# Row sums, the rounding of x and two weight conversions moved between engines in the start of a banded-attention and gated-FFN kernel

## The chip, the cores and the metric

The kernel runs on one core of one Trainium2 chip. The metric is the device time of one execution in microseconds (us), as the median of several runs. The core has five engines that each work through a queue of their own: TensorE (PE; its weight loads are shown apart as PEld), VectorE (DVE), ScalarE (ACT), GpSimd (POOL) and SyncE (SP), which here issues all DMAs.

## The reference

Attention over eight batches of 576 positions with eight heads of 64, in which each position sees itself and the 63 before it, and then a gated feed-forward network over the 4608 rows that come out:

```python
scores = 1 / np.sqrt(D) * np.matmul(q, k.transpose(0, 1, 3, 2))
rel = pos[:, None] - pos[None, :]
mask = (rel >= 0) & (rel < 64)
scores = np.where(mask, scores, -1000000000.0)
attn = np.exp(scores - np.max(scores, axis=-1, keepdims=True))
attn = attn / (np.sum(attn, axis=-1, keepdims=True) + 1e-09)
out = np.matmul(attn, v)                       # heads are put side by side: x is 4608 x 512
gate = 1.0 / (1.0 + np.exp(-(x @ w_gate)))     # 512 x 1536
return (gate * (x @ w_val)) @ w_out            # 1536 x 512
```

All weights come in as 64-bit numbers. The matrix products need more precision than one pass of the matrix engine gives, so every operand is split into a rounded high part and a low remainder, and each product is made of three matmuls: high by high, high by low, low by high.

## The kernel before

The 4608 rows are cut into 12 tiles of 384. A tile's attention is done in four units, one for each pair of heads: unit (t, p) is pair p of tile t. A unit goes through these steps:

- `scores` (line 224): 24 small matmuls into two banks, one for each head.
- `exponentials` (lines 235 to 260): six times VectorE adds the mask and takes the row's extreme (line 249), and ScalarE makes the exponential (line 257). For head 0 the exponential also accumulates its row sum; for head 1 of the first two tiles it doesn't.
- `normalize` (lines 267 to 274): for head 1 of the first two tiles VectorE sums the rows in an operation of its own (line 270); then it inverts the sums (lines 264 and 265), and GpSimd multiplies (line 274).
- `stage_b` (lines 319 to 333): TensorE transposes (line 324), and ScalarE copies the result out (line 329, tiles `pT0` and `pT1`).
- `stage_c` (lines 335 to 342): TensorE multiplies with v (line 354, tile `oo`); for the first two tiles `x_split` (lines 359 to 364) rounds the result to x's high part on ScalarE (line 361) and takes the low remainder on VectorE (line 362).

The weights come in slabs: number i is slab j, kind m of w_gate, w_val and w_out (0, 1, 2). A slab is loaded as 64-bit words by SyncE (`raw`, line 105). `conv_a` on ScalarE turns the high words into `w32` (line 117) and the low words, in place, into whole numbers (line 118). `conv_b` on VectorE puts the two together (lines 126 to 130). `conv_c` rounds the high part on ScalarE (line 158) and takes the remainder on VectorE (line 159), and SyncE stores the parts and `w32` for later tiles (lines 474 and 154). There are six buffers for `raw` and three for `w32`, so the fourth slab's `w32` can be written when the first one's store has been read out, and so on.

The first two tiles go through the network with their weights as these come (lines 376 to 440: `up` for the two products with x, at line 387, and `down` for the third, at line 435). The other ten tiles use a scheme with fewer products (line 612), which takes most of the time.

The order of the work is set in two steps. A list of events with due times (from line 731 on) fixes the order in which the program is written, and matmuls keep that order. A scheduler then orders each other engine's queue by its own forecast of when things are ready. `tc.issue_after(ins)` holds back what is written under it: it is queued behind `ins` on the engine on which `ins` itself stands, and on that engine alone. Lines 951 to 955 use this for the weights: slab 3 (gate, second) goes behind the two instructions that `x_split` noted for unit (1, 1), and slabs 2, 4 and 5 behind those of unit (1, 3) (`marks`, line 363). One of the two is the rounding at line 361, the other the remainder at line 362.

Of the kernel before, what the change touches and what calls it, by code (L numbers as in the profile page):

```python
# [14 lines left out]
AF = mybir.ActivationFunctionType  # L15
ALU = mybir.AluOpType
# [10 lines left out]
def attn_ffn(ctx: ExitStack, tc: tile.TileContext, qT, kT, vN, w_gate, w_val, w_out, out, outT):  # L27
# [3 lines left out]
    nc = tc.nc  # L31
# [56 lines left out]
    def table_order():  # L88
        return tc.issue_after(chain[-1]) if chain else nullcontext()
# [18 lines left out]
    def conv_a(i):  # L108


        j, m = divmod(i, KINDS)
        raw = conv[i]
        hw = raw.bitcast(F32).rearrange("p (n two) -> p n two", two=2)[:, :, 1]
        lw = raw.bitcast(U32).rearrange("p (n two) -> p n two", two=2)[:, :, 0]
        r32 = raw.bitcast(I32).rearrange("p (n two) -> p n two", two=2)[:, :, 0]
        w32 = mp.tile([P, DM], F32, name=f"w32_{m}_{j}", tag="w32", bufs=W32)
        nc.scalar.activation(w32, hw, AF.Copy, scale=2.0 ** -112)
        nc.scalar.activation(r32, lw, AF.Copy, scale=2.0 ** -29)
        conv[i] = (r32, w32)

    def conv_b(i):
# [107 lines left out]
    def softmax(t, p):  # L229
        sc = sc_of.pop((t, p))  # L230
        for h in range(2):
            exponentials(t, p, h, sc[h])
            normalize(t, p, h)

    def exponentials(t, p, h, sc):
        g0 = order[t] * UT
        if t < 2 and (NP * t + p) % 3 == 2:
            pt = mp.tile([P, TT], F32, name=f"p{h}_{t}_{p}", tag=("hh", "hl")[h], bufs=3)
            pt = pt.rearrange("p (u c) -> p u c", u=UP)
        else:  # L240
            pt = ap.tile([P, UP, P], F32, name=f"p{h}_{t}_{p}", tag="p", bufs=4)
        mn = sm.tile([P, UP], F32, name=f"mn{h}_{t}_{p}", tag="mn")
        if h == 0:
            sums_of[(t, p)] = sm.tile([P, 2, UP], F32, name=f"rs_{t}_{p}", tag="rs")
        rs = sums_of[(t, p)][:, h, :]
        for u in range(UP):
            key = [int((g0 + 2 * u + s) % SEQ == 0) for s in range(2)]
            key = tuple(key[::-1] if h else key)
            nc.vector.tensor_tensor_reduce(out=pt[:, u, :], in0=sc[u], in1=masks[key],  # L249
                                           op0=ALU.add, op1=ALU.min, scale=-SCALE, scalar=3.0e38,  # L250
                                           accum_out=mn[:, u:u + 1])
            with ExitStack() as behind:
                behind.enter_context(table_order())
                if NP * t + p - 2 in marks["pT"] and (t, p) != (1, NP - 1):
                    behind.enter_context(tc.issue_after(marks["pT"][NP * t + p - 2]))
                sums = {} if t < 2 and h else {"accum_out": rs[:, u:u + 1]}
                exp = nc.scalar.activation(pt[:, u, :], pt[:, u, :], AF.Exp, bias=mn[:, u:u + 1],  # L257
                                           scale=-1.0, **sums)
            chain.append(exp.ins)
        st[(t, p, h)] = pt  # L260

    def invert(rs):

        nc.vector.scalar_tensor_tensor(out=rs, in0=rs, scalar=2e-9, in1=rs, op0=ALU.add, op1=ALU.add)  # L264
        nc.vector.reciprocal(out=rs, in_=rs)  # L265

    def normalize(t, p, h):
        pt, rs = st[(t, p, h)], sums_of[(t, p)][:, h, :]
        if t < 2 and h:
            nc.vector.reduce_sum(out=rs, in_=pt, axis=mybir.AxisListType.X)  # L270
        if t < 4:
            invert(rs)
        eng = nc.vector if t == 3 and p % 2 or t // 2 == 2 else nc.gpsimd
        eng.tensor_mul(out=pt, in0=pt, in1=rs.unsqueeze(2).broadcast_to([P, UP, P]))  # L274
# [3 lines left out]
    def stage_s(t, p, done=None, spare=None):  # L278
        if done:
            sc = [a_bank(f"s{h}_{t}_{p}") for h in range(2)]  # L280
            sc_of[(t, p)] = [pieces(b) for b in sc]
            piece, start = spare_up(spare)
            oo = [sc[0][:, UP, :], sc[1][:, UP, :], piece]
            outputs(*done, oo, (True, True, start))
            x = xf_tile(*done).rearrange("p (u c) -> p u c", u=UP)
        scores(t, p)
        sc = sc_of.pop((t, p))
        if done:
            nc.scalar.copy(x[:, 2, :], oo[2])
            nc.scalar.copy(x[:, 1, :], oo[1])  # L290
        exponentials(t, p, 0, sc[0])
        if done:
            nc.scalar.copy(x[:, 0, :], oo[0])
        exponentials(t, p, 1, sc[1])
# [19 lines left out]
    def stage_n(t, p):  # L314
        invert(sums_of[(t, p)])
        for h in range(2):
            normalize(t, p, h)
# [17 lines left out]
    def stage_c(t, p):  # L335
        oo = bank(t, p, "o", f"oo_{t}_{p}")
        outputs(t, p, [oo[:, u, :] for u in range(UP)])
        oo = oo.rearrange("p u c -> p (u c)")
        if t < 2:
            xs[(t, p)] = x_split(oo, f"{t}_{p}", 4 * t + p, nc.vector)  # L340
        else:
            marks["xf"] = nc.scalar.copy(xf_tile(t, p), oo).ins
# [15 lines left out]

    def x_split(src, nm, i, eng):
        x2 = xp.tile([P, 2, TT], F32R, name=f"x_{nm}", tag=f"x{i}")  # L360
        hi = nc.scalar.copy(x2[:, 0, :], src)
        lo = eng.tensor_sub(out=x2[:, 1, :], in0=src, in1=x2[:, 0, :].bitcast(F32))  # L362
        marks[nm] = (hi.ins, lo.ins)
        return x2
# [146 lines left out]
    sums = {}  # L511
# [240 lines left out]
    for n in range(2 * NP):  # L752
        t, p = divmod(n, NP)
# [54 lines left out]
    for i in range(KINDS * NF):  # L808
        j, m = divmod(i, KINDS)
        tm = at[("up", 0, max(j, 1))] + ((-10, -2, 6 * j - 0.5) if j < 2 else (-9, -8, 2) if j == 2 else (-14, -12, 2))[m]  # L810
        if i < 2:
            tm = A0 + 11 + 8 * i
        else:
            put(tm - (30 if j == 0 or j == 1 and m < 2 else 6), 2.5, conv_load, i)
        put(tm, 1, conv_a, i)
        put(tm + 2.4, 2, conv_b, i)
        put(tm + (2.5 if i > 1 else 3.5), 2, conv_c, i)
# [115 lines left out]
    for i, (tm, o, f, a) in enumerate(events):  # L933
        if f in (conv_a, conv_b, conv_c):
            tm += late.get(a[0], 0.0)
            if f is not conv_b:
                wait = max([0.0] + [x + 0.05 - tm for x in freed if x - BEFORE < tm < x] + [x + 0.05 - tm for x in turned if x - 2 < tm < x])
                late[a[0]] = late.get(a[0], 0.0) + wait
                tm += wait
            events[i] = (tm, o, f, a)  # L940
    events.sort(key=lambda x: (x[0], x[1]))
    for tm, _, f, a in events:
        if f in (conv_a, conv_b, conv_c):
            with ExitStack() as behind:
                if f is not conv_b and any(x < tm < x + BEHIND for x in freed):
                    behind.enter_context(tc.issue_after(marks["xf"]))
                if f is not conv_b and any(x < tm < x + 8 for x in turned):
                    behind.enter_context(tc.issue_after(marks["pTv"]))
                j, m = divmod(a[0], KINDS)
                key = j - AHEAD if m < 2 else j - 1  # L950
                early = {3: ("1_1",), 2: ("1_3",), 4: ("1_3",), 5: ("1_3",)}.get(a[0], (key,))
                if j == 2 and m < 2:
                    early += tuple(("w", i) for i in (3, 4))
                for ins in [i for nm in early for i in marks.get(nm, ())]:
                    behind.enter_context(tc.issue_after(ins))
                if a[0] < 2:
                    behind.enter_context(tc.issue_after(marks["pT"][a[0] + (f is conv_c)]))
                f(*a)
        else:
            f(*a)  # L960
# [45 lines left out]
```

## Time and profile before

| what | value |
|---|---|
| three runs | 949.7, 950.18, 951.35 us; median 950.18 us |
| the profiled execution, its time | 948.82 us |
| its span, first to last instruction | 947.0 us |
| what lies around the span | 1.82 us |
| busy: PE, DVE, ACT, POOL | 933.2, 715.3, 501.7, 154.7 us |
| granted TensorE clock, whole span | 1.000 |

The profile is of one execution. Times in it are counted from the first instruction. An engine's row in the timeline gives the start, the duration, the engine, the line, the operation, and out<-in by tile names without their numbers; behind it, in brackets, stands the idle time before it and what ended it. Matmuls overlap each other, so a row of many is shorter than their sum. "SPq" rows are the issues of DMAs; when a DMA landed is the issue's start plus the time to landing, which the DMA view gives.

### The profile page before, as it was taken

How to read it: one execution, taken by the hardware profiler on the slowest of the kernel's cores; microseconds unless marked ns; L12 is line 12 of the kernel's file. 1: busy time of each engine (PE TensorE's matmuls, PEld its weight loads, DVE VectorE, ACT ScalarE, POOL GpSimd, SP SyncE). 2: the span in 40 equal slices, each digit the busy share in tenths (PEclk: the TensorE clock that was granted, in tenths of full speed). 3: DMA queues.
4: the chain of work that ended last, by engine and by line, in shares of the span. 5: the costliest groups of instructions: out<-in, count | busy, mean ns of one | idle time of the engine just before them, and what ended most of it. 6: DMA issues, size and time to landing. Idle time of an engine off the chain costs nothing.

```text
span 947.0 us, 20283 instructions
## 1 busy us (share of the span) xinstructions
PE 933.2 (99%) x7164; PEld 897.2 (95%) x7164; DVE 715.3 (76%) x1919; ACT 501.7 (53%) x1366; POOL 154.7 (16%) x232
## 2 busy tenths in 40 slices
PE   6999999999999999999999999999999999999998
PEld 5799999889999999999999999999999999999998
DVE  7999989887988975666875676786567796566882
ACT  7877566656666653555553555454455564222460
POOL 4211204604782000211000113000111100000000
PEclk9999999999999999999999999999999999999999
DMA  9999988989999989888889788789888688988464
GB/s 333 317 389 376 364 292 289 351 297 362 391 323 319 399 278 298 284 269 268 261 253 321 250 294 289 251 252 302 282 267 271 219 249 276 299 257 246 133 217 162
DMA packets 105509, 273.45 MB, mean 289 GB/s; under 512 B 11456, under 2 KB 33600, under 8 KB 105408
## 3 DMA queue, kind: packets, MB, share of 16 engines
q1 hardware_dynamic: 105408, 272.15, 85.2%
q8 instruction: 57, 0.93, 0.4%
q14 instruction: 44, 0.36, 0.1%
HBM read 220.20 MB, written 51.90 MB: 287 GB/s over the span
## 4 chain that ended last, share of the span: by engine, by line
PE 95%; DVE 2%; ACT 0%; issue 0%; DVEq 0%; ACTq 0%
PE pr L612 46%; PE y L612 23%; PE ph L387 10%; PE y L435 5%; PE pp L324 3%; PE pr L354 2%; PE s L224 1%; PE oo L354 1%; PE pr L224 1%; PE s L354 0%; DVE p L249 0%; DVE c L651 0%; DVE rs L264 0%; ACT p L257 0%; DVE x L362 0%; DVE rs L270 0%
## 5 line engine op out<-in xcount | busy, mean ns | idle before, releaser
L612 PE MATMUL pr<-x_T,wt 128*128 128x384 f32 x1224 | 224.4, 335 | 0.0
L612 PE MATMUL y<-h,wot 128*128 128x384 f32 x1260 | 220.4, 335 | 0.0
L612 PEld LDWEIGHTS y<-h,wot 128*128 128x128 f32 x1260 | 218.3, 188 | 1.3 <-DVE h L400 1.2
L612 PEld LDWEIGHTS pr<-x_T,wt 128*128 128x128 f32 x1224 | 212.5, 188 | 0.3 <-issue 0.3
L612 PE MATMUL pr<-x_B,wt 128*128 128x384 f32 x1008 | 188.7, 337 | 0.1
L612 PEld LDWEIGHTS pr<-x_B,wt 128*128 128x128 f32 x1008 | 174.4, 188 | 2.7 <-issue 2.1
L274 POOL TENSOR_TENSOR p<-p,rs 128x384 f32<-128x384 f32 x76 | 72.6, 971 | 521.3 <-DVE rs L265 359.9
L694 ACT CAST h<-h 128x384 fp32r<-128x384 f32 x210 | 104.8, 514 | 97.7 <-PE y L612 42.6
L695 DVE TENSOR_TENSOR h<-h,h 128x384 fp32r<-128x384 f32 x210 | 110.7, 556 | 23.1 <-ACT h L694 22.3
L257 ACT ACTIVATE p<-p,mn 128x128 f32<-128x128 f32 x288 | 110.7, 393 | 19.9 <-DVE mn L249 19.3
L387 PE MATMUL ph<-x,w 128*128 128x384 f32 x576 | 106.8, 339 | 0.1
L395 ACT ACTIVATE g<-c 128x384 f32<-128x384 f32 x90 | 47.0, 522 | 107.8 <-DVE c L651 96.0
L387 PEld LDWEIGHTS ph<-x,w 128*128 128x128 f32 x576 | 99.6, 188 | 2.6 <-issue 1.0
L622 DVE TENSOR_TENSOR c<-pr,p 128x384 f32<-128x384 f32 x60 | 33.1, 552 | 46.2 <-PE pr L612 46.2
L400 DVE SCALAR_TENSOR_TENSOR h<-g,c 128x384 f32<-128x384 f32 x90 | 50.5, 561 | 5.9 <-DVE c L651 0.5
L329 ACT COPY p<-pp 128x384 f32<-128x384 f32 x80 | 34.4, 479 | 35.0 <-PE pp L324 34.2
L257 ACT ACTIVATION_READ_ACCUMULATOR p<-p,mn 128x1 f32 x264 | 49.7, 188 | 0.0
L627 ACT COPY p<-pr 128x384 f32<-128x384 f32 x60 | 27.3, 474 | 37.9 <-PE pr L612 37.9
L622 DVE TENSOR_TENSOR u<-pr,p 128x384 f32<-128x384 f32 x60 | 33.1, 553 | 16.0 <-PE pr L612 15.7
L324 PE MATMUL pp<-ident,p 128*128 128x128 f32 x288 | 41.5, 279 | 2.2 <-POOL p L274 2.2
L651 DVE TENSOR_TENSOR c<-pr,p 128x384 f32<-128x384 f32 x60 | 33.2, 556 | 10.1 <-PE pr L612 9.7
L612 PE MATMUL pr<-x_T,ws 128*128 128x384 f32 x216 | 40.3, 338 | 0.0
(183 smaller groups left out, 1216.6 us busy)
## 6 DMA issues: line engine op xcount, KB each, us to landing
wt<-wd SPq DMA_DIRECT2D x186, 512.0 KB, 4.5
wot<-wod SPq DMA_DIRECT2D x105, 512.0 KB, 4.9
v<-in_vN_dram SPq DMA_DIRECT2D x48, 384.0 KB, 5.4
wd<-ws SPq DMA_DIRECT2D x48, 256.0 KB, 4.5
k<-in_kT_dram SPq DMA_DIRECT2D x48, 224.0 KB, 5.4
q<-in_qT_dram SPq DMA_DIRECT2D x48, 192.0 KB, 5.5
w32d<-w SPq DMA_DIRECT2D x36, 256.0 KB, 5.0
wd<-w SPq DMA_DIRECT2D x36, 256.0 KB, 5.8
```

What stands on the lines that cost most here:

```text
L257: exp = nc.scalar.activation(pt[:, u, :], pt[:, u, :], AF.Exp, bias=mn[:, u:u + 1], scale=-1.0, **sums)
L274: eng.tensor_mul(out=pt, in0=pt, in1=rs.unsqueeze(2).broadcast_to([P, UP, P]))
L324: pe(nc.tensor.transpose(pp[:, u, :], pt[:, u, :], ident))
L329: cp = nc.scalar.copy(pT, pp)
L387: pe(nc.tensor.matmul(ph, l, r, start=i == 0, stop=i == len(prs) - 1))
L395: act = nc.scalar.activation(g, c, AF.Tanh)
L400: nc.vector.scalar_tensor_tensor(out=out, in0=g, scalar=1.0, in1=val, op0=ALU.add, op1=ALU.mult)
L435: pe(nc.tensor.matmul(yb[y], l, r, start=first and n == 0, stop=last and n == 2))
L612: pe(nc.tensor.matmul(ps, l, r, start=first and i == 0, stop=last and i == 2, skip_group_check=not check))
L622: marks["plus"] = nc.vector.tensor_add(out=o, in0=ps, in1=a).ins
L694: nc.scalar.copy(h2[:, 0, :], src)
L695: nc.vector.tensor_sub(out=h2[:, 1, :], in0=src, in1=h2[:, 0, :].bitcast(F32))
```

## The change

Three things change, all of them in the first two tiles or the first two slabs:

- The exponentials of head 1 accumulate their row sums as well, and the sum on VectorE (line 270) is gone.
- x's high part is rounded on VectorE, not on ScalarE.
- The low words of slabs 0 and 1 are converted on GpSimd, not on ScalarE.

```diff
         nc.scalar.activation(w32, hw, AF.Copy, scale=2.0 ** -112)
-        nc.scalar.activation(r32, lw, AF.Copy, scale=2.0 ** -29)
+        if i < 2:
+            nc.gpsimd.tensor_scalar(out=r32, in0=lw, scalar1=2.0 ** -29, scalar2=None, op0=ALU.mult)
+        else:
+            nc.scalar.activation(r32, lw, AF.Copy, scale=2.0 ** -29)
...
-                sums = {} if t < 2 and h else {"accum_out": rs[:, u:u + 1]}
                 exp = nc.scalar.activation(pt[:, u, :], pt[:, u, :], AF.Exp, bias=mn[:, u:u + 1],
-                                           scale=-1.0, **sums)
+                                           scale=-1.0, accum_out=rs[:, u:u + 1])
...
-        if t < 2 and h:
-            nc.vector.reduce_sum(out=rs, in_=pt, axis=mybir.AxisListType.X)
...
-        hi = nc.scalar.copy(x2[:, 0, :], src)
+        hi = eng.tensor_copy(out=x2[:, 0, :], in_=src)
```

`eng` is VectorE in all calls. Behind the change line 118 has become line 119 (GpSimd) and 121 (ScalarE), and lines further down are shifted by a few. The scheduler orders the queues anew. TensorE's queue is the same in both kernels.

In ScalarE's queue before, from the first slab's rounding to the fourth unit's copies (a name like `pT0_0_2` is head 0, tile 0, pair 2; `w32_0_1` and `raw_0_1` are kind 0, slab 1; the last number only counts tiles):

```order
L158 CAST w0_0_479<-w32_0_0_402 128x2x256
L117 ACTIVATE w32_1_0_551<-raw_1_0_241 128x512
L118 ACTIVATE raw_1_0_241<-raw_1_0_241 128x512
L361 CAST x_0_1_498<-oo_0_1_485 128x384
L329 COPY pT0_0_2_505<-pp0_0_2_501 128x384
L329 COPY pT1_0_2_511<-pp1_0_2_507 128x384
L257 ACTIVATE p0_1_0_513,rs_1_0_515<-p0_1_0_513,mn0_1_0_514 128x128 x3
L257 ACTIVATE p1_1_0_525<-p1_1_0_525,mn1_1_0_526 128x128 x3
L158 CAST w1_0_624<-w32_1_0_551 128x2x256
L361 CAST x_0_2_567<-oo_0_2_554 128x384
L329 COPY pT0_0_3_578<-pp0_0_3_574 128x384
```

The same stretch in the changed kernel:

```order
L161 CAST w0_0_475<-w32_0_0_399 128x2x256
L117 ACTIVATE w32_1_0_546<-raw_1_0_241 128x512
L117 ACTIVATE w32_0_1_830<-raw_0_1_334 128x512
L121 ACTIVATE raw_0_1_334<-raw_0_1_334 128x512
L121 ACTIVATE raw_1_1_402<-raw_1_1_402 128x512
L329 COPY pT0_0_2_501<-pp0_0_2_497 128x384
L329 COPY pT1_0_2_507<-pp1_0_2_503 128x384
L259 ACTIVATE p0_1_0_509,rs_1_0_511<-p0_1_0_509,mn0_1_0_510 128x128 x3
L259 ACTIVATE p1_1_0_521,rs_1_0_511<-p1_1_0_521,mn1_1_0_522 128x128 x3
L121 ACTIVATE raw_2_0_424<-raw_2_0_424 128x512
L161 CAST w1_0_618<-w32_1_0_546 128x2x256
L117 ACTIVATE w32_1_1_895<-raw_1_1_402 128x512
```

The roundings of x have left ScalarE. Conversions of slabs 2, 3 and 4 (`raw_2_0`, `raw_0_1`, `raw_1_1`), which stood behind the second tile's roundings before, now stand among the units of the first tile: three ahead of the copies `pT0_0_2`, and one ahead of the copies of unit (0, 3). Further on in the same queue, before and behind the exponentials of unit (1, 1), it reads:

```order
L329 COPY pT0_0_3_573<-pp0_0_3_569 128x384
L329 COPY pT1_0_3_579<-pp1_0_3_575 128x384
L259 ACTIVATE p0_1_1_581,rs_1_1_583<-p0_1_1_581,mn0_1_1_582 128x128 x3
L259 ACTIVATE p1_1_1_593,rs_1_1_583<-p1_1_1_593,mn1_1_1_594 128x128 x3
L117 ACTIVATE w32_2_0_900<-raw_2_0_424 128x512
L121 ACTIVATE raw_2_1_898<-raw_2_1_898 128x512
L329 COPY pT0_1_0_644<-pp0_1_0_640 128x384
```

Two more conversions (slabs 2 and 5) have come ahead of `pT0_1_0`; before, only the rounding of x for unit (0, 3) stood there. In GpSimd's queue the changed kernel has, from the end of the first unit to the third (before, the same rows stand there without the two of line 119):

```order
L274 TENSOR_TENSOR p1_0_0_286<-p1_0_0_286,rs_0_0_276 128x384
L119 TENSOR_SCALAR raw_0_0_232<-raw_0_0_232 128x512
L274 TENSOR_TENSOR p0_0_1_311<-p0_0_1_311,rs_0_1_313 128x384
L274 TENSOR_TENSOR p1_0_1_323<-p1_0_1_323,rs_0_1_313 128x384
L119 TENSOR_SCALAR raw_1_0_241<-raw_1_0_241 128x512
L274 TENSOR_TENSOR p0_0_2_362<-p0_0_2_362,rs_0_2_364 128x384
L274 TENSOR_TENSOR p1_0_2_374<-p1_0_2_374,rs_0_2_364 128x384
```

The two conversions stand one ahead of the second unit's products and one ahead of the third's. In SyncE's queue the first 42 DMAs are the same ones in the same order in both kernels.

## The prediction

> **What bounds the kernel now.** I read the stretches first, then TensorE's waits, then the first 60 us of the timeline, engine by engine. The page and the stretches:
>
> ```profile
> span 947.0 us, 20283 instructions
> ...
> 0.00:25.00 25.00, 16.96 (x264) 13.23 (x264) 18.09 (x103) 19.18 (x64) 10.65 (x21) 1.00 0.93 335
> ...
> 50.00:75.00 25.00, 25.00 (x195) 22.96 (x194) 24.09 (x60) 19.30 (x43) 3.46 (x2) 1.00 1.03 383
> 200.00:947.00 747.00, 743.03 (x5547) 727.04 (x5545) 536.33 (x1388) 361.07 (x992) 98.38 (x152) 1.00 0.84 277
> ```
>
> The first numbers behind the length are TensorE's busy time. It idles 8 us in the first 25, none from 50 to 75, and 4 of the last 747. TensorE bounds all but the start. So what the start gains or loses goes straight to the end, unless a weight comes late. What TensorE waits for, whole span:
>
> ```profile
> PE s L224 <- DMA k<-in_kT_dram: 5.8, 3, 4.0
> PE pp L324 <- POOL p L274: 2.2, 4, 0.7
> PE oo L354 <- ACT pT L329: 1.2, 2, 0.6
> ```
>
> All of it is in the attention of the first two tiles. TensorE's timeline shows where the start ends:
>
> ```profile
> 38.41 2.04 PE L354 MATMUL oo<-pT,v 128*64 128x64 f32 x48 [0.64 <-ACT pT L329]
> 40.38 8.77 PE L387 MATMUL ph<-x,w 128*128 128x384 f32 x48
> ```
>
> At 40.38 the last units' outputs are done and the products with x begin, without idle time from there on. The question is where this 40.38 goes.
>
> **The change, part by part.** *ScalarE's queue.* This is the part that decides. An engine works through its queue in order: what stands ahead and waits holds up all behind it. The trace has such a case on ScalarE:
>
> ```profile
> 49.91 0.67 ACT L117 ACTIVATE w<-raw 128x512 f32<-128x512 f32 x1 [1.75 <-DMA w32d<-w]
> ```
>
> A conversion stood idle for 1.75 us until a store had read out the `w32` buffer that it writes. The rounding of x has left ScalarE, and with it the instruction behind which the conversions of slabs 2 to 5 were queued there. In the changed order, three of them (the high words of slab 3, then the low words of slabs 3 and 4) stand ahead of the copies `pT0_0_2`; `w32_1_1`, which needs the first slab's `w32` buffer, stands ahead of `pT0_0_3`; `w32_2_0`, which needs the second's, and the low words of `raw_2_1` stand ahead of `pT0_1_0`. TensorE needs these copies for its next matmuls, and all later units' exponentials are queued behind them. So I ask when each DMA lands. SyncE's issues:
>
> ```profile
> 20.10 0.33 SPq L105 DMA_DIRECT2D raw<-in_moe_w_gate_dram  x1
> 21.09 0.33 SPq L105 DMA_DIRECT2D raw<-in_moe_w_val_dram  x1
> 21.57 0.46 SPq L105 DMA_DIRECT2D raw<-in_moe_w_out_dram  x1
> ...
> 26.46 0.33 SPq L154 DMA_DIRECT2D w32d<-w  x1
> ...
> 31.46 0.32 SPq L154 DMA_DIRECT2D w32d<-w  x1
> 32.03 0.33 SPq L105 DMA_DIRECT2D raw<-in_moe_w_out_dram  x1
> ```
>
> These are the loads of slabs 3, 4 and 2, the stores of slabs 0 and 1, and the load of slab 5. The DMA view, asked for the windows 20.0 to 21.6, 26.4 to 26.6 and 31.4 to 32.2 us, gives the time to landing:
>
> ```profile
> raw<-in_moe_w_gate_dram SPq DMA_DIRECT2D x1, 512.0 KB, 6.3
> raw<-in_moe_w_val_dram SPq DMA_DIRECT2D x1, 512.0 KB, 6.5
> raw<-in_moe_w_out_dram SPq DMA_DIRECT2D x1, 512.0 KB, 7.3
> ...
> w32d<-w SPq DMA_DIRECT2D x1, 256.0 KB, 7.3
> ...
> raw<-in_moe_w_out_dram SPq DMA_DIRECT2D x1, 512.0 KB, 6.1
> w32d<-w SPq DMA_DIRECT2D x1, 256.0 KB, 5.4
> ```
>
> So they land at 26.4, 27.6 and 28.9, the stores at 33.8 and 36.9, the last load at 38.1. Will the change move them? From 2 to 37 us the DMA engines are full:
>
> ```profile
> 2.00:37.00 35.00, 28.09 (x403) 22.65 (x404) 28.82 (x154) 27.74 (x100) 15.36 (x21) 1.00 1.01 370
> ```
>
> (1.01 is their share.) SyncE's queue is the same in this stretch, so I keep the times. The prices on ScalarE:
>
> ```profile
> 24.48 0.86 ACT L329 COPY pT<-pp 128x384 f32<-128x384 f32 x2
> 25.22 0.42 ACT L257 ACTIVATE p<-p,mn 128x128 f32<-128x128 f32 x1
> ...
> 32.08 0.40 ACT L257 ACTIVATE p<-p,mn 128x128 f32<-128x128 f32 x1 [1.17 <-DVE mn L249]
> ...
> 34.51 0.83 ACT L329 COPY pT<-pp 128x384 f32<-128x384 f32 x2
> ...
> 36.72 0.71 ACT L117 ACTIVATE w<-raw 128x512 f32<-128x512 f32 x1
> ...
> 37.87 1.61 ACT L329 COPY pT<-pp 128x384 f32<-128x384 f32 x4
> ...
> 57.03 0.40 ACT L257 ACTIVATE p<-p,mn 128x128 f32<-128x128 f32 x1
> ...
> 59.35 0.66 ACT L117 ACTIVATE w<-raw 128x512 f32<-128x512 f32 x1
> ```
>
> From start to start: two copies 0.74 (24.48 to 25.22); two conversions 1.15 (36.72 to 37.87), so 0.58 each; six exponentials that all accumulate 2.32 (57.03 to 59.35, a unit of the third tile). The walk:
>
> - Slab 3 lands at 26.4; its two conversions end at 27.6; slab 4 has landed; its low words end at 28.2. The copies `pT0_0_2` start there; before, those of the unit after it started at 24.48.
> - Copies 0.74, exponentials of unit (1, 0) 2.32: 31.3. Two more operations of at most 0.7: 32.7. The next conversion waits for the store at 33.8 and ends at 34.4. `pT0_0_3` starts, 9.9 later than its 24.48.
> - Copies and exponentials of unit (1, 1), 3.06: 37.4. The store has landed at 36.9; conversion: 38.0. The load lands at 38.1; low words: 38.7. Then `pT0_1_0`; copies and exponentials of (1, 2): 41.8.
> - VectorE must invert and give the extremes of unit (1, 3). Before, that took from the end of the exponentials, where the sum starts, to ScalarE's 32.08, 1.5 us:
>
> ```profile
> 30.55 0.55 DVE L270 TENSOR_REDUCE rs<-p 128x3 f32<-128x384 f32 x1
> ```
>
> Without the sum 1.0 is left: 42.8. Exponentials 2.32: 45.1; copies `pT0_1_1`, 0.83: 45.9.
> - Before, these copies ended at 35.34, and TensorE reached the products at 40.38: 5.04. Two conversions of slab 3 (1.15) stood in between and are done by then: 3.9. The products start at 49.8, against 40.38: **9.4 us late**.
>
> *x on VectorE.* Eight roundings come to it and eight sums go. The sum's 0.55 is above. What rounding from the matrix results costs there no row shows; the nearest are these two:
>
> ```profile
> 36.05 0.36 DVE L413 CAST hh<-h 128x384 fp32r<-128x384 f32 x1
> ...
> 37.44 0.55 DVE L362 TENSOR_TENSOR x<-oo,x 128x384 fp32r<-128x384 f32 x1
> ```
>
> One is the same operation from the other memory, the other a subtraction from the same place: 0.36 to 0.55, and I take 0.45. At the first units the held-up ScalarE hides it. At unit (1, 3) nothing does: TensorE needs its low part at the eleventh product, 1.8 us behind the start (48 of them in 8.77). VectorE then has four operations on x (two at 0.45, two at 0.55) and two on slab 3 (0.7 each at most) from the end of unit (1, 2)'s outputs, 1 us ahead of the start: 3.4 at most, so 0 to 0.6 late. I take **0.3**.
>
> *Sums in the exponentials.* Priced in the walk; the six cost 2.32.
>
> *Low words on GpSimd.* The second one stands ahead of unit (0, 2)'s products and waits for its load:
>
> ```profile
> 9.54 0.33 SPq L105 DMA_DIRECT2D raw<-in_moe_w_val_dram  x1
> ...
> raw<-in_moe_w_val_dram SPq DMA_DIRECT2D x1, 512.0 KB, 8.5
> ...
> 14.45 0.83 POOL L274 TENSOR_TENSOR p<-p,rs 128x384 f32<-128x384 f32 x1 [0.37 <-DVE rs L265]
> ```
>
> It lands at 18.0; before, the products began at 14.45. No row shows this conversion on GpSimd. For 512 numbers a row, by the product's 0.83 for 384, it is 1.1; below, ScalarE's 0.67; above I allow twice the product's rate, 2.2. With two products of 0.83 and the transposes (0.9) it is over by 22.8 at most; the copies don't start before 28.2. It costs nothing, by 5 us. Without that cover the products would begin at 19.1 for 14.45, up to 4.7 later.
>
> The sum is 9.4 + 0.3 = 9.7. The profiled execution took 948.82, so 958.5 by this; it lay 1.36 under the median of 950.18, which becomes **959.9 us**. No stall is left at the end of the walk that could give it back: behind 40.38 TensorE has nothing to catch up with. How far the landings can stray, the view of the tile `raw` in the first 62 us shows:
>
> ```profile
> DMA to landing us min/median/max: 5.6/6.5/8.5
> ```
>
> With 8.5 for the last load the sum is 2.4 more (962.3). With the first store landing as fast as the second (5.4), ScalarE itself decides and the sum is 1.1 less (958.8); with x on VectorE for nothing, 958.5.
>
> **The rivals.** *(a) The conversions are ready in time and the change gains.* ScalarE would meet slab 3 at about 20 us (24.48 less a unit's copies, exponentials and conversions, some 4), so it must land 6 us earlier than 26.4; from there on every microsecond of landing counts. Then eight sums less (4.4) and eight roundings more (2.9 to 4.4) on VectorE, which leads the start's chain, give up to 1.5: 948.7 us, faster than before but inside what can be told. More is hardly there. Against it: DMA engines full to 37 us, and the same issues.
>
> *(b) TensorE slows after its long wait.* With `pT0_0_2` at 28.2 TensorE has nothing to do for some 5 us, and some 3 us before `pT0_0_3`. The same 24 matmuls early and later:
>
> ```profile
> 11.51 1.56 PE L224 MATMUL s<-k,q 64*64 64x128 f32 x24
> ...
> 20.22 0.89 PE L224 MATMUL s<-k,q 64*64 64x128 f32 x24 [0.98 <-DMA k<-in_kT_dram]
> ```
>
> The first stretch, with pauses, ran 0.67 slower each time, at a granted clock that the rows give as 1.00 all through. If this comes back and holds to the end of the start, four such groups of the walk's last part (the scores of (1, 3), the outputs of (1, 1), (1, 2) and (1, 3)) are each 0.67 slower: 2.7, and 962.6 us. [...]
>
> That the change does not do what it says is excluded by the order: the instructions stand there.
>
> **How the numbers follow.** The walk, with landings as they were or a little off (958 to 962.3): 0.78, and its 959.9 us is the forecast. (b): 0.15, at 960.5 to 963. (a): 0.07, most of it, 0.04, within 0.2% and 0.03 faster than that; 0.2%, 1.9 us, is about the spread of the runs of before (949.7 to 951.35) and what can be told from no change. Slower by more: 0.93. The range leaves out (a) and the outer end of (b): 957.5 to 963.
>
> **What would show it.** In the changed profile: ScalarE idle some 6 to 7 us until 26.4, ended by a load of `raw`, at line 117; idle again about 1 us until 33.8, ended by a `w32d` store; `pT` copies at 28.2, 34.4 and 38.7; the 48 products at line 387 starting at 49 to 50.5, and no idle time of TensorE behind. Line 361 on VectorE at 0.36 to 0.55. Wrong, if the products start before 45 (the loads came earlier, or the queue doesn't hold), or if TensorE idles behind 50 (a weight is late, which I have not counted).

## The result and the profile after

| what | before | after |
|---|---|---|
| median of four runs each | 950.76 us (949.7 to 951.65) | 960.65 us (959.62 to 961.13) |
| the profiled execution, its time | 948.82 us | 960.62 us |
| its span | 947.0 us | 958.6 us |

The ratio is 1.0106, with a 95% interval of 1.0094 to 1.0118: the changed kernel is 1.1% slower, about 10 us. The two profiled spans differ by 11.6, because the profiled execution of before lay 1.9 under its median and that of after at it.

ScalarE's timeline of the changed kernel (start, duration, line, out<-in; in brackets the idle time ahead and what ended it), the exponentials left out:

```profile
18.98 0.66 ACT L117 ACTIVATE w<-raw 128x512 f32<-128x512 f32 x1
26.16 0.66 ACT L117 ACTIVATE w<-raw 128x512 f32<-128x512 f32 x1 [6.52 <-DMA raw<-in_moe_w_gate_dram]
26.72 1.36 ACT L121 ACTIVATE raw<-raw 128x512 int32<-128x512 uint32 x2
27.99 0.84 ACT L329 COPY pT<-pp 128x384 f32<-128x384 f32 x2
...
33.55 0.66 ACT L117 ACTIVATE w<-raw 128x512 f32<-128x512 f32 x1 [1.35 <-DMA w32d<-w]
34.12 0.84 ACT L329 COPY pT<-pp 128x384 f32<-128x384 f32 x2
37.16 0.66 ACT L117 ACTIVATE w<-raw 128x512 f32<-128x512 f32 x1
37.97 0.67 ACT L121 ACTIVATE raw<-raw 128x512 int32<-128x512 uint32 x1
38.54 0.84 ACT L329 COPY pT<-pp 128x384 f32<-128x384 f32 x2
...
44.77 0.83 ACT L329 COPY pT<-pp 128x384 f32<-128x384 f32 x2
```

ScalarE is idle for 6.5 us in front of a conversion whose load has not landed, and 1.35 in front of one whose buffer has not been read out. The copies that TensorE needs stand right behind: at 27.99, 34.12 and 38.54. What TensorE makes of it:

```profile
20.78 0.90 PE L324 MATMUL pp<-ident,p 128*128 128x128 f32 x3 [3.38 <-POOL p L274]
...
28.50 1.93 PE L354 MATMUL oo<-pT,v 128*64 128x64 f32 x24 [4.09 <-ACT pT L329]
...
34.63 1.29 PE L354 MATMUL oo<-pT,v 128*64 128x64 f32 x24 [1.33 <-ACT pT L329]
...
49.66 2.33 PE L387 MATMUL ph<-x,w 128*128 128x384 f32 x10
52.62 6.86 PE L387 MATMUL ph<-x,w 128*128 128x384 f32 x38 [0.63 <-DVE x L362]
```

The 48 products begin at 49.66, where they began at 40.38 before, and stop once more behind the tenth for a remainder of x. Ahead of the long wait there is another, of 3.38 us, for GpSimd. Its timeline:

```profile
11.86 1.56 POOL L119 TENSOR_SCALAR raw<-raw 128x512 int32<-128x512 uint32 x1 [1.96 <-DMA raw<-in_moe_w_gate_dram]
13.50 1.64 POOL L274 TENSOR_TENSOR p<-p,rs 128x384 f32<-128x384 f32 x2
17.75 2.07 POOL L119 TENSOR_SCALAR raw<-raw 128x512 int32<-128x512 uint32 x1 [2.61 <-DMA raw<-in_moe_w_val_dram]
19.90 4.26 POOL L274 TENSOR_TENSOR p<-p,rs 128x384 f32<-128x384 f32 x4
```

Both traces hold the same 7164 matmuls in the same order, so each can be paired with its twin. How late it starts against before, in us, for eight of them (the first column is the start in before), in the changed kernel and in the experiments that follow:

| start in before, and what | after | no hold | x alone | no GpSimd | slab 5 | slab 2 |
|---|---|---|---|---|---|---|
| 17.41, transposes of (0, 2) | 3.37 | -0.07 | -0.32 | 0.10 | 0.44 | 0.04 |
| 21.03, outputs of (0, 2) | 7.47 | 7.45 | 7.04 | 7.67 | -0.09 | 0.01 |
| 25.01, outputs of (0, 3) | 9.62 | 9.14 | 8.52 | 9.18 | -0.07 | 5.58 |
| 29.32, products, tile 0 | 9.83 | 8.72 | 9.08 | 9.39 | 8.94 | 6.56 |
| 40.38, first of the 48 products | 9.28 | 8.97 | 7.95 | 8.63 | 10.71 | 5.77 |
| 42.38, behind its last remainder | 10.24 | 9.24 | 9.21 | 9.60 | 10.75 | 5.79 |
| 64.99, transposes of (2, 0) | 10.99 | 10.32 | 9.99 | 10.90 | 10.73 | 5.77 |
| 237.97, products with `wt` | 11.53 | 10.83 | 11.44 | 12.23 | 12.20 | 7.89 |
| end | 11.57 | 10.87 | 11.39 | 12.22 | 12.19 | 7.88 |

### The profile page after: what moved, and what is told of

It reads as the page before. It is cut to its first block, busy times and chain, and to the rows that moved or that the text cites. A ratio compares the mean times of both kernels' runs of the same rounds, so it can differ in the third digit from the quotient of the medians.

```text
span 958.6 us, 20299 instructions
## 1 busy us (share of the span) xinstructions
PE 935.1 (98%) x7164; PEld 897.9 (94%) x7164; DVE 715.2 (75%) x1919; ACT 499.4 (52%) x1380; POOL 156.6 (16%) x234
## 4 chain that ended last, share of the span: by engine, by line
PE 90%; DMA 5%; DVE 2%; ACT 1%; issue 1%; SPq 0%; POOL 0%; DVEq 0%; POOLq 0%; ACTq 0%
PE pr L612 45%; PE y L612 23%; PE ph L387 8%; PE y L435 5%; PE pp L324 3%; PE pr L354 2%; DMA k<-in_kT_dram 1%; PE s L227 1%; DMA raw<-in_moe_w_val_dram 1%; DMA w32d<-w 1%; PE oo L354 1%; DMA wt<-wd 1%; PE pr L227 1%; DMA raw<-in_moe_w_out_dram 1%; DMA q<-in_qT_dram 1%
## 5 line engine op out<-in xcount | busy, mean ns | idle before, releaser
L622 DVE TENSOR_TENSOR c<-pr,p 128x384 f32<-128x384 f32 x60 | 33.1, 551 | 45.9 <-PE pr L612 45.8
L259 ACT ACTIVATION_READ_ACCUMULATOR p<-p,mn 128x1 f32 x288 | 54.4, 189 | 0.0
L627 ACT COPY p<-pr 128x384 f32<-128x384 f32 x60 | 27.1, 472 | 36.9 <-PE pr L612 36.9
L324 PEld LDWEIGHTS pp<-ident,p 128*128 128x128 f32 x288 | 34.6, 144 | 9.3 <-POOL p L274 7.0
```

What stands on the lines that cost most here:

```text
L324: pe(nc.tensor.transpose(pp[:, u, :], pt[:, u, :], ident))
L622: marks["plus"] = nc.vector.tensor_add(out=o, in0=ps, in1=a).ins
```

## The experiments

Theory A, the prediction's: the roundings of x were what the weight conversions were held behind on ScalarE. With them on VectorE nothing holds the conversions; they stand early in ScalarE's queue and make it wait for DMAs. Theory B, the rival: the moved work itself costs, on VectorE, on GpSimd or on ScalarE, wherever the conversions stand. All times are set against the kernel before on the same chip. Its medians there were 949.45 us (for no hold, the hold put back, and parts 1 and 2 alone), 949.75 (for part 3 alone, the held change without part 3, the sums with the first tile's x, and slab 5) and 949.97 (for the other three).

**No hold, nothing moved.** The kernel before, with the mark on ScalarE left out:

```diff
-        marks[nm] = (hi.ins, lo.ins)
+        marks[nm] = (lo.ins,)
```

> The kernel before, with no work moved: the rounding of x is only left out of the marks behind which slabs 2 to 5 are queued. Theory A: ScalarE waits for slab 3's load until about 26.3, for the stores until about 33.6 and 37, the products start at 49 to 51 us and the time is 959 to 962 us. Theory B: as the kernel before, 950 to 951.5 us.

Measured: 959.37 us, ratio 1.0109 (1.0094 to 1.0124). This kernel does the very work of before on the very engines of before, and has the whole loss. Its ScalarE and TensorE:

```profile
25.94 0.66 ACT L117 ACTIVATE w<-raw 128x512 f32<-128x512 f32 x1 [5.79 <-DMA raw<-in_moe_w_gate_dram]
...
27.97 0.84 ACT L329 COPY pT<-pp 128x384 f32<-128x384 f32 x2
...
33.62 0.86 ACT L329 COPY pT<-pp 128x384 f32<-128x384 f32 x2
...
37.88 0.87 ACT L329 COPY pT<-pp 128x384 f32<-128x384 f32 x2
```

```profile
28.48 1.92 PE L354 MATMUL oo<-pT,v 128*64 128x64 f32 x24 [8.01 <-ACT pT L329]
...
49.35 2.03 PE L387 MATMUL ph<-x,w 128*128 128x384 f32 x10
```

The copies start within 0.7 us of the changed kernel's (27.99, 34.12, 38.54), the products within 0.3.

**The change with a hold put back.** The marks take in the instruction of the copies as well:

```diff
-        marks[nm] = (hi.ins, lo.ins)
+        marks[nm] = (hi.ins, lo.ins, marks["pTv"])
```

> The changed kernel, with the conversions of slabs 2 to 5 queued again behind ScalarE's copies of units (1, 1) and (1, 3). Theory A (the order in ScalarE's queue, which then waits for DMAs in the middle of the units, costs the time): no idle time of 6.5 us on ScalarE before line 117, the products start at 40 to 43.5 us, and the time is 950 to 953.5 us; not all the way to the kernel before, since GpSimd's wait for the second slab's load (its products began 3.4 us later than before) is no longer hidden. Theory B (the work that was moved to VectorE and GpSimd costs the time by itself): the products start at 49 to 50 us and the time stays at 959 to 961.

Measured: 953.27 us, ratio 1.0042 (1.0026 to 1.0059). The work is moved as in the change, and some 6 of the 10 us are gone. The products begin at 40.69, 0.3 later than before. What remains comes mostly later: the lateness is 0.8 behind the last remainder of x, 2.9 at 115 us and 4.2 at 238.

**Part 1 alone, the sums.** All else as before:

```diff
-                sums = {} if t < 2 and h else {"accum_out": rs[:, u:u + 1]}
...
-                                           scale=-1.0, **sums)
+                                           scale=-1.0, accum_out=rs[:, u:u + 1])
...
-        if t < 2 and h:
-            nc.vector.reduce_sum(out=rs, in_=pt, axis=mybir.AxisListType.X)
```

> The kernel before with the first part alone: head 1's sums by the exponentials, the VectorE sum gone. Both theories: it moves nothing in ScalarE's queue. By the walk, 0.55 us less on VectorE for each of eight units and 0.25 us more on ScalarE: the products start 0 to 2 us earlier than at 40.4, and the time is 949 to 951 us.

Measured: 949.87 us, ratio 1.0006 (0.9997 to 1.0016): no difference that can be told. The time is in the range of the text on record, but its earlier start isn't there: the products begin at 40.98, 0.6 later than before, though VectorE is rid of eight sums.

**Part 2 alone, x on VectorE.** All else as before:

```diff
-        hi = nc.scalar.copy(x2[:, 0, :], src)
+        hi = eng.tensor_copy(out=x2[:, 0, :], in_=src)
```

> The kernel before with the second part alone: x rounded on VectorE. Theory A: this part alone undoes the hold, so the products start at 49 to 51 us and the time is 959 to 962 us, about all of the change. Theory B, by rows: eight roundings of 0.55 us on VectorE, 4.4 us at most: 951 to 955 us.

Measured: 960.26 us, ratio 1.0116 (1.0101 to 1.0132). The one line that takes the hold away makes the whole loss.

**Part 3 alone, GpSimd.** The first hunk of the change's diff, all else as before.

> Only the third part of the change: the low words of the first two slabs go through GpSimd, everything else is as before, ScalarE's later conversions are held back as before. Theory A (the order of ScalarE's queue makes the loss): products of line 387 start at 40 to 41 us as before, and the time is that of the kernel before but for the wait that GpSimd's two conversions put ahead of its probability products, 0 to 3 us: 949.5 to 953. Theory B (the moved work itself costs): the two conversions take 1.6 to 2.1 us each on GpSimd and delay the products of unit (1,0) and later by 3 us or more: 953 to 956.

Measured: 950.55 us, ratio 1.0012 (1.0003 to 1.0021): 0.8 us. TensorE does wait, and gets a part back. Its waits, and GpSimd's two conversions, in this kernel (the lines are 3 further down here):

```profile
PE pp L327 <- POOL p L277: 5.1, 6, 2.5
```

```profile
12.41 1.57 POOL L119 TENSOR_SCALAR raw<-raw 128x512 int32<-128x512 uint32 x1 [1.87 <-DMA raw<-in_moe_w_gate_dram]
...
17.53 1.96 POOL L119 TENSOR_SCALAR raw<-raw 128x512 int32<-128x512 uint32 x1 [1.86 <-DMA raw<-in_moe_w_val_dram]
```

TensorE is 3.0 us late at 17.41 and 1.4 at 40.38, so the products begin at 41.8; the time is in theory A's range, the start of the products is above its 40 to 41.

**The change without part 3.** The low words of slabs 0 and 1 stay on ScalarE, nothing is held:

```diff
-        if i < 2:
-            nc.gpsimd.tensor_scalar(out=r32, in0=lw, scalar1=2.0 ** -29, scalar2=None, op0=ALU.mult)
-        else:
-            nc.scalar.activation(r32, lw, AF.Copy, scale=2.0 ** -29)
+        nc.scalar.activation(r32, lw, AF.Copy, scale=2.0 ** -29)
```

> The changed kernel without its third part: all low words stay on ScalarE, which is still not held. It tells whether GpSimd's two conversions, which kept TensorE waiting 3.4 us at 17.4 us in the changed kernel, cost anything there. Theory A: the wait for the load at 26.1 us covers them, the probabilities' copies start at 28 us all the same, and the time is within 0.6 us of the changed kernel's: 960 to 961.3. If they cost their wait, 957 to 958. The granted clock should then show no half speed before TensorE's long wait itself.

Measured: 961.28 us, ratio 1.0119 (1.0104 to 1.0135), no faster than the changed kernel (1.0106). GpSimd's 3.38 us cost nothing there. As the text expected, the granted clock shows no half speed ahead of TensorE's long wait: that wait begins at 20.1, and the clock falls at 23.4. ScalarE waits for the same load with or without them:

```profile
26.36 0.66 ACT L117 ACTIVATE w<-raw 128x512 f32<-128x512 f32 x1 [5.77 <-DMA raw<-in_moe_w_gate_dram]
```

**The change held, without part 3.** The edits of the held kernel and of the last one together.

> The changed kernel without its third part, with ScalarE's conversions held back again by the copies of the probabilities. Beside the run with the third part and the same hold (953.3) it tells whether its 3.8 us over the kernel before come from GpSimd or from the rounding of x on VectorE. If GpSimd: 949 to 950.5, products of line 387 from 40.4 us, and no losses of 0.5 us or more at 50 to 250 us. If the rounding on VectorE (0.55 us each, ahead of the remainders that the products wait for): 951.5 to 953.5, with the same steps of the shift behind 50 us. Theory A wants less than 955 of it in both cases.

Measured: 951.92 us, ratio 1.0026 (1.0014 to 1.0037). So of the held kernel's loss GpSimd's part made about 1.5 us (1.0042 against 1.0026, whose intervals overlap), and the rest some 2.2. The time lies in the range that the text gave for the rounding on VectorE; that this is the whole of the 2.2 isn't shown. Here the products begin earlier than before, the only such kernel of the series:

```profile
39.48 2.34 PE L384 MATMUL ph<-x,w 128*128 128x384 f32 x10
41.97 6.88 PE L384 MATMUL ph<-x,w 128*128 128x384 f32 x38
```

The 0.9 us won at 40.38 are given back soon: 0.6 late at 65, 1.8 at 115, 2.7 at 191. The waits of TensorE that are new from 50 us on are small ones, 0.8 us in all for `xf` on ScalarE and 0.3 to 0.4 each for operations of VectorE; they don't add up to the whole.

**x on VectorE for the first tile, with the sums.** The second tile's roundings stay on ScalarE, and with them the hold. (The text on record counts the third part among what stays; this kernel leaves it out, its low words are all on ScalarE.) Against the changed kernel, beside the edit of the one without part 3:

```diff
-        hi = eng.tensor_copy(out=x2[:, 0, :], in_=src)
+        hi = eng.tensor_copy(out=x2[:, 0, :], in_=src) if i < 4 else nc.scalar.copy(x2[:, 0, :], src)
```

> The change with the rounding of x put on VectorE for the first tile alone; the third part of the change and the sums stay. The second tile's roundings are on ScalarE, so that they hold ScalarE's conversions as before. Theory A: products of line 387 at 40 to 41.5 us, time 949 to 952.5. Theory B: the three parts' work is nearly all still moved, so nearly all of the loss stays: 956 to 960.

Measured: 950.43 us, ratio 1.0004 (0.9995 to 1.0012): the time of before. Four of the eight roundings and all the sums are moved, and nothing is lost.

**x on VectorE for the first tile, alone.** The same edit of line 361 in the kernel before, sums as before.

> The only one of the change's moves that the hold survives, by itself: the rounding of x on VectorE for the first tile, nothing else. Four casts of 0.47 us leave ScalarE, 0.55 us each come to VectorE, before 40 us. Theory A: no wait is new, so 949 to 950.8, within 0.2% of the kernel before; if ScalarE's work before 40 us were the bound it could gain up to 1.9 us: 947.9.

Measured: 951.71 us, ratio 1.0018 (1.0010 to 1.0027), 1.7 us over before and above what theory A gave for it. There is a cost of the moved work after all: TensorE is 1.0 late at 25.01 and 2.0 at 29.32. The first 1.0 can be followed. Ahead of the copies of unit (0, 3) ScalarE rounds a slab of weights, and VectorE must first have put that slab together. In the kernel before:

```profile
23.58 0.62 ACT L158 CAST w<-w 128x512 fp32r<-128x512 f32 x1 [0.23 <-DVE w L130]
```

In this kernel:

```profile
24.93 0.62 ACT L158 CAST w<-w 128x512 fp32r<-128x512 f32 x1 [1.62 <-DVE w L130]
```

The copies behind ScalarE's wait start at 25.46, where they started at 24.48. With the eight sums gone from VectorE as well (the kernel ahead) the wait is 0.56, and the lateness is 0.0 and 0.5. VectorE's load as a whole doesn't tell these kernels apart: from 2 to 40 us it was busy 31.52 us in the kernel before, 31.77 here, 29.05 in the kernel ahead, and 28.11 with the sums alone, where the products came no earlier. What differs is what VectorE has ahead of this one piece of work: the rounding of x, 0.53, and then line 128, which takes 1.19 where it took 0.69. The other 1.0 was not followed.

**One slab's hold taken away: slab 5.** The kernel before, no work moved; only the low words of slab 5 lose their hold on ScalarE:

```diff
         marks[nm] = (hi.ins, lo.ins)
+        marks[nm + "_v"] = (lo.ins,)
...
-                early = {3: ("1_1",), 2: ("1_3",), 4: ("1_3",), 5: ("1_3",)}.get(a[0], (key,))
+                early = {3: ("1_1",), 2: ("1_3",), 4: ("1_3",), 5: ("1_3_v",)}.get(a[0], (key,))
```

> The kernel before, no work moved, and the hold taken from one slab alone, the sixth: its low words' conversion of 0.67 us may now stand in ScalarE's queue ahead of the copy of the first probabilities of the second tile's first unit, and its load landed at 38.1 us in the changed kernel. Theory A (an instruction that waits in an in-order queue costs its wait, whatever its own length): the copies behind it start at 38.5 to 39, the products of line 387 at 47 to 50, and the time is 956 to 960. Theory B (cost is what the moved work takes): one conversion moved by 0.67 us leaves 949.5 to 951.

Measured: 960.96 us, ratio 1.0121 (1.0107 to 1.0135). In ScalarE's queue one instruction has changed its place among the first two tiles:

```profile
26.31 0.98 ACT L257 ACTIVATE p<-p,mn 128x128 f32<-128x128 f32 x3
37.18 0.65 ACT L118 ACTIVATE raw<-raw 128x512 int32<-128x512 uint32 x1 [9.89 <-DMA raw<-in_moe_w_out_dram]
37.74 0.46 ACT L361 CAST x<-oo 128x384 fp32r<-128x384 f32 x1
38.10 0.86 ACT L329 COPY pT<-pp 128x384 f32<-128x384 f32 x2
```

0.65 us of work, 9.89 of waiting, 11 in the result. This is the plainest answer to theory B. Up to 29 us this kernel runs nearly as before (0.4 us late at 17.41, 0.1 early at 21.03 and 25.01); it loses all at once what the changed kernel loses in three steps, because both must wait for the same last load.

It loses more than theory A said: the time is 1 us above its 956 to 960, and the products begin at 51.09, not at 47 to 50. (The 38.1 in the text is that load's landing in the kernel before; in the changed kernel it landed at 37.89.) TensorE's rows say where: behind its wait the matmuls are slow.

```profile
38.25 1.33 PE L388 MATMUL ph<-x,w 128*128 128x384 f32 x3 [8.84 <-ACT x L361]
39.51 1.56 PE L224 MATMUL s<-k,q 64*64 64x128 f32 x24
41.00 1.55 PE L354 MATMUL oo<-pT,v 128*64 128x64 f32 x24
42.48 1.54 PE L324 MATMUL pp<-ident,p 128*128 128x128 f32 x6
```

In the kernel without any hold the same three groups, at 39.38 to 41.04, took 0.89, 0.92 and 0.87. The lateness here grows from 8.94 at the first product behind the wait to 11.12 at 32.55 of before. The windows' PEclk column, third from the end, has the reason:

```profile
34.00:40.00 6.00, 1.75 (x13) 1.28 (x17) 0.56 (x1) 2.82 (x10) 0.00 (x0) 0.50 0.62 239
40.00:44.00 4.00, 4.00 (x52) 3.55 (x48) 2.87 (x19) 3.11 (x14) 1.66 (x2) 0.50 0.01 4
44.00:50.00 6.00, 5.31 (x67) 4.62 (x67) 4.79 (x11) 4.45 (x12) 1.66 (x2) 1.00 0.00 0
```

Half the clock was granted to 44 us, 5.8 behind the wait's end. Of the 2.2 us lost to it, 0.4 are won back by the first of the 48 products (10.71).

**One slab's hold taken away: slab 2.** The same with another slab, whose load lands 9 us earlier:

```diff
-                early = {3: ("1_1",), 2: ("1_3",), 4: ("1_3",), 5: ("1_3",)}.get(a[0], (key,))
+                early = {3: ("1_1",), 2: ("1_3_v",), 4: ("1_3",), 5: ("1_3",)}.get(a[0], (key,))
```

> A dose: the kernel before, no work moved, with the hold taken from the third slab alone (index 2) in place of the sixth. Its low words' conversion, again one instruction of 0.67 us, then stands behind the exponentials of the second tile's first unit, which ended at 23.3 us where the sixth slab's hold was gone, and its load landed at 28.7 to 28.9 us. Theory A (the cost is the wait for the load, from the point where ScalarE's queue gets there): a wait of 5 to 5.5 us, all behind it 5 to 5.7 us late, products of line 387 at 45.4 to 46.5, time 954.5 to 956.5, about half of what the sixth slab cost. Theory B (the cost is the moved work, or any loss of the hold): either 949.5 to 951 or, as for the sixth slab, about 961.

Measured: 956.71 us, ratio 1.0068 (1.0055 to 1.0080). ScalarE, and the products on TensorE:

```profile
28.62 0.65 ACT L118 ACTIVATE raw<-raw 128x512 int32<-128x512 uint32 x1 [5.21 <-DMA raw<-in_moe_w_out_dram]
```

```profile
46.16 6.17 PE L388 MATMUL ph<-x,w 128*128 128x384 f32 x33
```

The wait is 5.21 where 5 to 5.5 was expected, the products 5.8 late. The same 0.65 us of work costs 6.7 us here and 11.2 with slab 5. What it costs is the time for which it waits. The median lies 0.2 above the range, by what is lost far behind: the lateness is 5.8 up to 115 us and 7.9 at 238, where TensorE waits 1.1 us for a weight.

No kernel of the series is faster than before. Nearest to it come the sums alone and the sums with the first tile's x, whose intervals hold 1.

## Why the prediction was right

**What bounds it.** Right, nearly: a loss at the start goes to the end. Of 9.28 late at the products 11.57 became; nothing was given back.

**The walk.** Right in its mechanism and in each time. Forecast and measured: the conversion that waits for slab 3 starts at 26.4 / 26.16; the copies at 28.2 / 27.99, 34.4 / 34.12 and 38.7 / 38.54; the copies of unit (1, 1) at 45.1 / 44.77; the products at 49.8 / 49.66, so 9.4 / 9.28 late. That the landings stay was right too: 26.14 for slab 3, 33.47 and 36.64 for the stores, 37.89 for slab 5. That this queue makes the loss is shown: without the hold and with no work moved there are 9.9 us (959.37 against 949.45), and with one instruction misplaced 11.2 (960.96 against 949.75). The three waits are not additive. In the kernel with slab 5 alone the first two are missing, and the products are no earlier. In the changed kernel itself ScalarE comes to the last load only 0.2 us too early: the next conversion could have started at 37.7 (0.57 behind that of 37.16) and starts at 37.97.

One side sum of the prediction doesn't follow from its own walk. With the first store landing sooner it takes 1.1 us off. But ScalarE would then be through with unit (1, 1) at 36.3 and would still meet the second store at 36.9 and the last load at 38.1. The copies would start at 38.7 all the same, and nothing would come off.

**x on VectorE.** The mechanism was right, the size too small: 0.3 was forecast, and the lateness grows by 0.96 at the eleventh product (9.28 to 10.24). Two numbers were off. One cast took not 0.45 but the upper bound:

```profile
L361 DVE CAST x<-oo x8: 544/545/553, 17.3 to 51.0; 128x384 fp32r<-128x384 f32 x8
```

(ns, smallest, median, largest.) From the matrix results (PSUM) the cast took 0.55, against the 0.36 of the row in the prediction from the other memory (SBUF). The prediction's own rows could have given this: the remainder's 0.55 reads the same place. The other number is the start. VectorE didn't come to its six operations 1 us ahead of the products, but 0.24 ahead, behind two operations on the weights:

```profile
48.37 0.41 DVE L129 TENSOR_SCALAR zz<-w 128x512 int32<-128x512 int32 x1
48.81 0.69 DVE L131 SCALAR_TENSOR_TENSOR w<-w,zz 128x512 int32<-128x512 int32 x1
49.42 0.55 DVE L361 CAST x<-oo 128x384 fp32r<-128x384 f32 x1
...
52.02 0.55 DVE L362 TENSOR_TENSOR x<-oo,x 128x384 fp32r<-128x384 f32 x1
```

**Low words on GpSimd.** Right that they cost nothing here: without them the loss is no smaller (ratio 1.0119 against 1.0106). The price of one was too low: 1.56 and 2.07 us against 1.1, inside the bounds of 0.67 and 2.2. So the products of unit (0, 2) began at 19.90 in the changed kernel, 5.5 later than the 14.45 of before, where the prediction's account without the cover had up to 4.7. Less of it reaches TensorE and the end: the transposes came 3.4 us late, and part 3 by itself costs 0.8 us.

**"No stall behind the walk."** Wrong for 1.3 us against the trace of before, the only step of the sum that failed outright: from 10.24 at 42.38 the lateness grows to 11.57. In TensorE's waits, whole span:

```profile
PE oo L354 <- ACT pT L329: 6.6, 4, 4.1
PE pp L324 <- POOL p L274: 5.7, 6, 3.4
...
PE pr L612 <- DMA wt<-wd: 0.7, 1, 0.7
```

The last row, at 249 us, is a weight that came late, which the prediction named as a thing not counted. The lateness takes a step between 191 and 238 us in every kernel of the series but the held one without part 3, from 0.4 to 1.6 us: 0.6 here, 1.1 in the kernel with the sums alone, 1.6 with slab 2. All of them are counted against one trace of the kernel before, of an execution that lay under its median. So the step may belong to that execution as much as to the change. The DMA engines are full around there (a share of 1.02 from 220 to 250). That the DMA time lost early causes it (a share of 0.08 from 37 to 50 us, against 0.80 before) was not tested; it stays open, and so does the step of 0.75 between 42 and 65 us.

So by the sum 9.7 stood against 11.6 between the two profiled spans, and 959.9 against 960.65 between the medians. The second distance is smaller because the profiled execution of before, at 948.82, lay under all four of its runs, by 1.9 under their median. The sum was too small by the same 1.9 (0.7 for x, 1.3 behind the walk, less 0.1 in the walk), so that the medians come out so close, 9.9 apart for a sum of 9.7, is in part luck.

**Rival (a), the conversions ready in time and a gain.** Its condition did not come, and earlier loads were not tried, since the DMA engines are full (a share of 1.01 to 1.05 from 16 to 34 us in the changed kernel). The held kernels take the same wait away, and they don't bear out its price: not 1.5 us faster than before, but 3.8 slower with GpSimd's part and 2.2 without it. VectorE's relief does show, as products 0.9 us earlier, and is lost again behind.

**Rival (b), TensorE slowed by its long wait.** Matmuls at half the clock were measured, but the price did not come here. In the changed kernel:

```profile
16.00:20.00 4.00, 1.40 (x46) 1.09 (x36) 3.93 (x20) 3.64 (x15) 2.17 (x2) 0.93 1.05 385
20.00:24.00 4.00, 2.89 (x30) 2.16 (x30) 4.00 (x12) 0.00 (x0) 4.00 (x4) 0.50 1.05 388
24.00:28.00 4.00, 0.41 (x8) 0.01 (x1) 0.71 (x1) 1.77 (x4) 0.16 (x1) 0.50 1.01 395
28.00:34.00 6.00, 4.80 (x54) 3.95 (x54) 3.32 (x19) 4.65 (x18) 1.66 (x2) 0.58 1.03 385
34.00:40.00 6.00, 4.46 (x42) 3.57 (x42) 3.43 (x19) 5.85 (x23) 1.66 (x2) 1.00 0.65 242
```

From 19.4 to 33.1 us half the clock was granted, and the 24 outputs at 28.50 took 1.93 where those at 34.63 took 1.29. It cost nothing: until 33.55 the store that ScalarE waits for sets the pace, and by then the clock was back. So it didn't hold to the end of the start, as the rival's price had it. The fall at 19.4 came 2.0 us into the wait of 3.38, and the clock returned behind 4.6 us of work without a pause; with slab 5 it returned behind 5.8. A long wait is not all that goes ahead of a fall. In the kernel with slab 5 the clock also fell at 16.7, and in that with slab 2 at 21.2, where TensorE's waits behind its first one (for `k`, 3.9 and 4.0 us) had all been below 0.9; half clock lasted 3.4 us each time. What makes it fall was not shown. What half the clock costs where nothing covers it is in the kernel with slab 5: 2.2 us, since its wait is the last one.

## What to carry to other kernels

An instruction that was moved to another engine no longer held back what was ordered behind it on the old one, and that alone made the loss here (960.26 us with part 2 alone, 959.37 with the mark left out, against 949.45); before moving one, look for who uses it as a mark. What an instruction put too early in ScalarE's queue cost here was in the main the landing of its input less the time at which the queue got there, whatever its own length: 0.65 us of work cost 6.7 or 11.2 us, with waits of 5.2 and 9.9. And the costs of such waits, each taken alone, didn't add up where they stood in a row for DMAs that came in a fixed order: 6.7 (slab 2) and 11.2 us (slab 5) alone, 9.9 with no hold at all. The last one decided here, and what else went wrong ahead of it in the changed kernel, a conversion of 2.07 us on GpSimd or half the clock from 19.4 to 33.1, was free.

## What the runs showed of the hardware

- Granted clock: it fell to 0.50 during waits of TensorE of 3.4 us (changed kernel) and 8.8 (slab 5), 2.0 and 4.4 us after they began, and came back behind 4.6 and 5.8 us of matmuls without a pause. It also fell, for 3.4 us, where TensorE's waits behind its first had all been below 0.9 us (slab 5 at 16.7, slab 2 at 21.2). It cost 2.2 us of TensorE's time with slab 5, where work waited for it.
- GpSimd's conversion of 512 numbers a row, every second 32-bit word read and written in place, took 1.56 to 2.07 us, against 0.64 to 0.71 on ScalarE; GpSimd's product of 384 took 0.83 in most rows of the start.
- VectorE's cast of 384 numbers a row out of the matrix results took 0.54 to 0.55 us in the changed kernel, no less than a subtraction from there (0.54 to 0.56); ScalarE's took 0.46 to 0.49 in the kernel before.
